# Attention scores as three float16 products instead of one float32 product, in a fused three-layer kernel

## The chip, the cores and the metric

One core of a Trainium2 chip runs the whole program. The metric is the device time of one execution in microseconds (us). The engines are TensorE (PE, with its weight loads listed as PEld), VectorE (DVE), ScalarE (ACT), GpSimd (POOL) and SyncE (SP), which issues the DMAs.

## What is computed

Three layers in a row, on 8 x 576 tokens of 512 features. First an attention in chunks of 64 tokens, 8 heads of 64; then a feed-forward layer; then a gated layer that mixes tokens. The first one, on which the change acts:

```python
scores = scale * np.matmul(q_c, k_c.transpose(0, 1, 2, 4, 3))
scores = scores - np.max(scores, axis=-1, keepdims=True)
attn = np.exp(scores)
attn = attn / (np.sum(attn, axis=-1, keepdims=True) + 1e-09)
out = np.matmul(attn, v_c)
```

The second layer normalizes a row of the result, multiplies by `w_ch1` (512 x 2048), applies a ReLU, multiplies by `w_ch2` (2048 x 512) and adds the row. The third does `w_in`, a GELU, a gate with `w_sg`, and `w_out`.

## The kernel before

Tokens are in 36 tiles of 128 rows, here called units, t = 0 to 35; two units make a block of the feed-forward layer (18 blocks). The program has two parts. The first does attention and feed-forward, block after block; its order comes from `Plan`: every operation is entered with an engine, a duration, what it reads and writes, a priority and a latency for its readers, and `Plan.run` lists them greedily, each engine at its earliest moment and by priority. What it lists is then the fixed order of each engine's queue; at run time each instruction waits on semaphores. The second part (the gated layer) has a plan of its own.

Operations with `two=1` hold off operations of the other engine of the pair DVE and POOL that carry `two` as well: the planner never lets a marked one of POOL overlap a marked one of DVE.

From unit 10 on (`JOIN`) attention runs inside the feed-forward blocks of two blocks earlier. Big matmuls are written as three float16 products of halves: high by high, high by low, low by high, where ACT rounds to the high half and DVE (or POOL) subtracts to get the low half. So it is with the second product of attention from unit 10 on (`pv_`, L341 to L356: 48 matmuls of 64x64). The scores, however, are float32: `scores` (L279) loads Q and K of a unit into `qkl` (one buffer, 128 x 1024 float32, L283), and `qk` (L286) issues 16 matmuls of 64x64, four at a time in the four quarters of TensorE. For units 10 to 34 `attention` enters `pv_` of unit t and `qk` of unit t+1 as one operation (L429), called a burst below; the scores of unit 10 stand alone (L317), and the second product of unit 35 does (L425).

Around a burst in the attention of a unit: the row maximum (L389) and the subtraction (L390) on DVE straight from PSUM, the exponential on ACT (L393), its high half (L400, ACT) and low half (L401, DVE), a DMA that transposes both halves (`ptt`, L404), the halves of V (`vq`, L408 ACT, L409 DVE), row sums (L413, L377, L378), then the next burst. After it, L430 scales the result into `x`, and `norm` (L439) normalizes it (L462, L463, POOL L457 and L460, L466), halves it into `hl` (L469 ACT, L471 POOL) and transposes it by DMA to `xT` (L267).

The feed-forward work in between, one of 8 steps of a block: 24 matmuls into a bank (`ff1p`, L750), a ReLU out of it on ACT (L765), sums on DVE (L772 to L774), the high half on ACT (L777), the low half on DVE (L778), and two steps later 21 matmuls (`ff2p`, L802) whose third one is the first to read the low half. At a block's end DVE (L825) and POOL (L835) add up the results. Between these the planner spreads the conversion of the third layer's weights (L491, L924, L987 on DVE), at the lowest priority.

Of the kernel before, what the change touches and what calls it, by code (L numbers as in the profile page):

```python
# [9 lines left out]
F16 = mybir.dt.float16  # L10
F32 = mybir.dt.float32
# [3 lines left out]
AF = mybir.ActivationFunctionType  # L15
ALU = mybir.AluOpType
# [8 lines left out]
    a=[2264, -1991, -1698, -26, -1734, 4025, 2562, -374],  # L25
# [4 lines left out]
    lo=[1, 0, 0, 0, 0, 1, 1, 1],  # L30
# [8 lines left out]
    xn=[0, 1, 0, 0, 1, 1, 1, 1],  # L39
    g=[150, 12000, 200, 400, 150],  # L40
    f=[-277, -1680, 2543],
# [9 lines left out]
JOIN = 10  # L51
# [96 lines left out]
def fused_kernel(ctx: ExitStack, tc, qkv, w1, w2, g1, w_in, w_out, wsgt, wsgs, g2, b_sg, out):  # L148
    nc = tc.nc
    PSUM = bass.MemoryType.PSUM  # L150
    P = 128
# [64 lines left out]
    op = plan.op  # L216
# [54 lines left out]
    def palloc(tag, bufs, shape, dt, pool=None):  # L271
        return plan.buf(tag, bufs, lambda: (pool or pools["att"][1]).tile(shape, dt, tag=tag, name=tag, bufs=bufs))
# [3 lines left out]
    started = {}  # L276
    BYDMA = 10

    def scores(t, o):  # L279

        a = palloc("qk", 2, [P, 2, 512], F32) if t < JOIN else palloc("qkl", 1, [P, 2, 512], F32)
        src = qkv[t].rearrange("p (a f) -> p a f", a=3)
        o("SP", 1700, lambda: nc.sync.dma_start(out=a.t, in_=src[:, 0:2]), wr=[a], lat=2200 if t < JOIN else 4000)  # L283
        s2 = pair[t % 2 if t < 6 else 1]

        def qk():  # L286
            for hp in range(4):
                for r in (slice(0, 64), slice(64, 128)):
                    for c in range(2):
                        k = hp * 128 + c * 64  # L290
                        nc.tensor.matmul(  # L291
                            s2[64 * c:64 * c + 64, r.start // 64, hp * 64:hp * 64 + 64],
                            lhsT=a.t[r, 0, k:k + 64],
                            rhs=a.t[r, 1, k:k + 64],
                            start=True,
                            stop=True,
                        )

        started[t] = a, qk

    def attention(t):
        n = t % 2 if t < 6 else 1
        s2, ks = pair[n], f"pair{n}"
        kp = ks if t < JOIN else "pairv"
        pr = TUNE['a'][t] if t < 8 else 10 * t
        lat = TUNE['g'][2] if t < 8 else 300 if t < JOIN else 600 if t < JOIN + 2 else 1000 if t < BYDMA else 400
        far = dict(lat=1500 if t < JOIN + 2 else 3000 if t < BYDMA else 1000) if t >= JOIN else {}
        z = 1

        def o(eng, ns, fn, **k):  # L310
            ns = FAST.get((eng, ns), ns)
            op(eng, ns, fn, prio=k.pop("prio", pr), lat=k.pop("lat", lat), **k)

        if t not in started:
            scores(t, o)
            a, qk = started[t]
            o("PE", 1260 * z, qk, rd=[a], wr=[ks])  # L317
        v = palloc("v", 2, [P, 512], F32) if t < JOIN else palloc("vl", 1, [P, 512], F32)
        o("SP", 730, lambda: nc.sync.dma_start(out=v.t, in_=qkv[t].rearrange("p (a f) -> p a f", a=3)[:, 2]), wr=[v], lat=2200)
        mx = palloc("mx", 2, [P, 2, 4, 1], F32)  # L320
        pm = palloc("pm", 2, [P, 4, 2, 64], F32) if t < JOIN else palloc("pml", 1, [P, 4, 2, 64], F32)
        sm = palloc("sm", 2, [P, 4, 2, 1], F32)
        rd = palloc("rd", 2, [P, 4, 2, 1], F32)
        pt = palloc("pt", 1, [P, 4, 128], F32) if t < BYDMA else None
# [7 lines left out]
        ptt, vq = [None], [None]  # L332
        pp = lambda: [pt, v] if t < BYDMA else [ptt[0], vq[0]]
# [7 lines left out]
        def pv_():  # L341
            if t >= BYDMA:
                for hp in range(4):
                    for n, (y, z) in enumerate(((0, 0), (0, 1), (1, 0))):
                        for r in (slice(0, 64), slice(64, 128)):
                            for c in range(2):
                                k = c * 256 + hp * 64
                                q = hp * 128 + c * 64
                                nc.tensor.matmul(  # L349
                                    s2[64 * c:64 * c + 64, r.start // 64, 256 + hp * 64:256 + hp * 64 + 64],  # L350
                                    lhsT=ptt[0].t[r, y, q:q + 64],
                                    rhs=vq[0].t[r, z, k:k + 64],
                                    start=(n == 0),
                                    stop=(n == 2),
                                )
                return  # L356
            for hp in range(4):
                for r in (slice(0, 64), slice(64, 128)):
                    for c in range(2):
                        k = c * 256 + hp * 64  # L360
                        nc.tensor.matmul(
                            s2[64 * c:64 * c + 64, r.start // 64, 256 + hp * 64:256 + hp * 64 + 64],
                            lhsT=pt.t[r, hp, 64 * c:64 * c + 64],
                            rhs=v.t[r, k:k + 64],
                            start=True,
                            stop=True,
                        )
# [12 lines left out]
        def sums():  # L380
# [10 lines left out]
            out=pm.t.rearrange("p h a k -> p a h k"), in0=sv, in1=mx.t.to_broadcast([P, 2, 4, 64]), op=ALU.subtract  # L391
# [4 lines left out]
        else:  # L396
            ph = palloc("ph", 1, [P, 2, 512], F16)
# [4 lines left out]
                out=ph.t[:, 1], in0=flat(), in1=ph.t[:, 0], op=ALU.subtract  # L402
            ), rd=[pm], wr=[ph], two=1)
            o("SP", 1100, lambda: nc.sync.dma_start_transpose(  # L404
                out=ptt[0].t.rearrange("p x (h q) -> p (x h) q", h=4), in_=ph.t.rearrange("p x f -> p (x f)")
# [4 lines left out]
                out=vq[0].t[:, 1], in0=v.t, in1=vq[0].t[:, 0], op=ALU.subtract  # L410
# [4 lines left out]
        if t < BYDMA:  # L415
            o("ACT", 480, lambda: nc.scalar.activation(
                out=pt.t.rearrange("p (a h) q -> p a h q", a=2),
                in_=s2[:, :, 0:256].rearrange("p a (h q) -> p a h q", h=2),
                func=AF.Copy,
# [4 lines left out]
        if t < JOIN or t + 1 == NT:  # L424
            o("PE", 1260 * z, pv_, rd=pp(), wr=[kp])  # L425
        else:
            scores(t + 1, o)
            a_, qk_ = started[t + 1]
            o("PE", 1260, lambda: (pv_(), qk_()), rd=pp() + [a_], wr=[kp, ks])  # L429
        o("DVE", 600, lambda: nc.vector.tensor_tensor(  # L430
            out=x.t.rearrange("p (h a d) -> p a h d", h=4, a=2),
            in0=pv,
            in1=rd.t.rearrange("p h a o -> p a h o").to_broadcast([P, 2, 4, 64]),
# [5 lines left out]
    def norm(t, x, o):  # L439

        bs = palloc("bs", 2, [P, 6], F32)
        mv = palloc("mv", 2, [P, 2], F32)
        rs = palloc("rs", 2, [P, 1], F32)
        xn = palloc("xn", 1, [P, 512], F32)
        hl = palloc("hl", 2, [P, 2, 512], F16)
        b = t // 2
        c0 = (t % 2 if b < B0 else 1 - t % 2) * 128
        if t % 2 == 0:
            if b == 2:
                xT_t[b] = plan.buf("xT2", 1, lambda: stage.tile([P, 2, 4, 256], F16, name="xT2"))  # L450
            else:
                xT_t[b] = palloc("xT", 2, [P, 2, 4, 256], F16, px)
        xT = xT_t[b]
        x_t[t] = x

        def rs_():
            nc.gpsimd.tensor_scalar(  # L457
                out=rs.t, in0=mv.t[:, 1:2], scalar1=1.0, scalar2=1e-6, op0=ALU.mult, op1=ALU.add
            )
            nc.gpsimd.tensor_tensor(out=rs.t, in0=rs.t, in1=cpow, op=ALU.pow)  # L460

        o("DVE", 600, lambda: nc.vector.bn_stats(out=bs.t, in_=x.t), rd=[x], wr=[bs])  # L462
        o("DVE", 70, lambda: nc.vector.bn_aggr(out=mv.t, in_=bs.t), rd=[bs], wr=[mv])  # L463
        o("POOL", 730, rs_, rd=[mv, "cpow"], wr=[rs], two=2)
        xe = ("POOL", 830, nc.gpsimd) if t < 8 and TUNE['xn'][t] else ("DVE", 460, nc.vector)
        o(xe[0], xe[1], lambda: xe[2].tensor_scalar(  # L466
            out=xn.t, in0=x.t, scalar1=mv.t[:, 0:1], scalar2=rs.t, op0=ALU.subtract, op1=ALU.mult
        ), rd=[x, mv, rs], wr=[xn], two=1 + (xe[0] == "POOL"))
        o("ACT", 520, lambda: nc.scalar.activation(out=hl.t[:, 0], in_=xn.t, func=AF.Copy), rd=[xn], wr=[hl])  # L469
        lo = ("DVE", 600, nc.vector) if t < 8 and TUNE['lo'][t] else ("POOL", 1110, nc.gpsimd)  # L470
        o(lo[0], lo[1], lambda: lo[2].tensor_tensor(  # L471
            out=hl.t[:, 1], in0=xn.t, in1=hl.t[:, 0], op=ALU.subtract
        ), rd=[xn], wr=[hl], two=1)
        o("SP", 1100, lambda: transpose(xT.t, slice(c0, c0 + 128), hl.t), rd=[hl], wr=[xT], lat=2200)
# [379 lines left out]

    bW = {"top": Buf("topB", None)}

    ATT = [f"{n}{k}" for n in ("qk", "v", "mx", "pm", "sm", "rd", "bs", "mv", "rs", "hl") for k in range(2)] + ["pt", "xn", "qkl", "vl", "u0", "u1", "pml", "ph", "ptt", "vq"]
    w2s = {}

    def open_sums():  # L860
# [822 lines left out]
```

## Time and profile before

| | us |
|---|---|
| median of 3 runs | 1175.69 (1175.21 to 1175.86) |
| the profiled execution's own time | 1174.16 |
| its span, first to last instruction | 1172.4 |
| PE busy in the span | 1160.4 (99%) |
| DVE, ACT, POOL busy | 921.5, 587.8, 200.6 |

The profiled execution took 1.53 us (0.13%) less than the median of the runs. A busy share is an average over stages; a wait counts only where the engine that waits is the one that sets the end. In the rows, a duration of a matmul overlaps the next one's, so what a batch of matmuls costs is read from the start of the batch to the start of what follows it.

### The profile page before, as it was taken

The page shows a single profiled execution, that of the slowest core. Times are in us where ns is not written, and L with a number is a line of the kernel's source. Part 1 is how long each engine was busy: PE and PEld are TensorE (multiplying, and loading weights), DVE is VectorE, ACT ScalarE, POOL GpSimd, SP SyncE. Part 2 cuts the span into 40 slices and gives each one's busy share as a digit, 9 for nine tenths or more (in the row PEclk, how much of TensorE's full clock was granted, in tenths as well). Part 3 has the DMA queues.
Part 4 walks back from the last instruction along what each step waited for, and adds up shares of the span by engine and source line. Part 5 has one row for each costly group of instructions (what it writes and reads, how often), then busy time and mean ns, then how long its engine had stood idle before and what let it go on. Part 6 is the DMA issues. An engine that isn't in the chain of part 4 may idle for free.

```text
span 1172.4 us, 28060 instructions
## 1 busy us (share of the span) xinstructions
PE 1160.4 (99%) x11858; PEld 880.5 (75%) x11858; DVE 921.5 (79%) x1752; ACT 587.8 (50%) x858; POOL 200.6 (17%) x279
## 2 busy tenths in 40 slices
PE   7999999999999999999999999999999999999998
PEld 5787448888888888888888888888565566556454
DVE  6997887989998998768877865677889579577455
ACT  5777635656565644434444443345646445434330
POOL 2211010212312222311311222012102001102100
PEclk8999999999999999999999999999999999999999
DMA  8973018454333444233233211436275463362203
GB/s 299 284 233 113 18 28 256 147 127 67 79 89 77 104 115 101 55 77 92 56 91 74 61 41 37 98 78 176 42 139 164 107 145 110 94 121 72 91 1 117
DMA packets 169278, 125.42 MB, mean 107 GB/s; under 512 B 132928, under 2 KB 142016, under 8 KB 169152
## 3 DMA queue, kind: packets, MB, share of 16 engines
q1 hardware_dynamic: 169152, 123.63, 40.5%
q8 instruction: 93, 1.52, 0.5%
q14 instruction: 33, 0.27, 0.1%
HBM read 72.74 MB, written 18.88 MB: 78 GB/s over the span
## 4 chain that ended last, share of the span: by engine, by line
PE 93%; DVE 3%; DMA 2%; ACT 1%; issue 1%; POOL 0%; SPq 0%; ACTq 0%; DVEq 0%; POOLq 0%
PE bank L750 25%; PE acc L802 22%; PE pb L1478 5%; PE bank L638 5%; PE acc L1562 4%; PE pair L659 4%; PE pb L1562 4%; PE acc L1478 3%; PE pb L1382 3%; PE pb L1424 3%; PE acc L1424 3%; PE acc L1382 3%; PE bank L659 2%; PE pair L291 2%; PE pair L349 1%; DMA xT<-hl 1%
## 5 line engine op out<-in xcount | busy, mean ns | idle before, releaser
L750 PE MATMUL bank<-xT,w1h 128*128 128x256 f16 x1920 | 320.9, 273 | 0.0
L802 PEld LDWEIGHTS <-arena 128*128 128x128 f16 x2520 | 244.1, 98 | 31.0 <-DVE arena L778 1.2
L750 PE MATMUL bank<-xT,w1l 128*128 128x256 f16 x960 | 261.8, 273 | 0.0
L802 PE MATMUL acc<-w,arena 128*128 128x256 f16 x1440 | 218.3, 273 | 0.6 <-DVE arena L778 0.6
L750 PEld LDWEIGHTS <-w1h 128*128 128x128 f16 x1920 | 187.7, 98 | 22.1
L777 ACT ACTIVATE arena<-arena 128x896 f16<-128x896 f32 x120 | 113.9, 949 | 144.1 <-PE acc L802 67.6
L802 PE MATMUL acc<-w2s,arena 128*128 128x256 f16 x1080 | 177.2, 273 | 0.0
L778 DVE TENSOR_TENSOR arena<-arena 128x896 f16<-128x896 f32 x120 | 132.1, 1101 | 36.7 <-ACT arena L777 36.4
L765 ACT ACTIVATE arena<-bank 128x512 f32<-128x512 f32 x120 | 71.3, 594 | 127.0 <-PE bank L750 124.0
L750 PEld LDWEIGHTS <-w1l 128*128 128x128 f16 x960 | 93.9, 98 | 10.9
L835 POOL TENSOR_TENSOR x<-x,u 128x256 f32<-128x256 f32 (+1 forms) x65 | 63.2, 998 | 174.9 <-ACT arena L777 107.7
L772 DVE TENSOR_TENSOR arena<-arena 128x256 f32<-128x256 f32 x120 | 57.2, 477 | 34.3 <-ACT arena L765 33.2
L1562 PEld LDWEIGHTS <-w2s 128*128 128x128 f16 x444 | 43.4, 98 | 47.3
L1382 PEld LDWEIGHTS <-x2T 128*128 128x128 f16 x672 | 65.5, 98 | 9.8
L638 PE MATMUL bank<-xT,w1h 128*128 128x256 f16 x384 | 64.4, 273 | 1.1 <-DMA xT<-hl 0.8
L457 POOL TENSOR_SCALAR rs<-mv 128x1 f32<-128x1 f32 x36 | 11.0, 306 | 312.9 <-DVE mv L463 283.5
L1424 PEld LDWEIGHTS <-late 128*128 128x128 f16 x336 | 32.7, 98 | 39.2
L773 DVE TENSOR_TENSOR arena<-arena 128x256 f32<-128x256 f32 x120 | 56.0, 467 | 4.1
L471 POOL TENSOR_TENSOR hl<-xn,hl 128x512 f16<-128x512 f32 x32 | 45.1, 1410 | 80.1 <-ACT hl L469 80.1
L1478 PEld LDWEIGHTS <-vh 128*128 128x128 f16 x288 | 28.6, 99 | 33.3
L1562 PE MATMUL acc<-wout,w2s 128*128 128x512 f16 (+1 forms) x252 | 53.3, 369 | 0.0
L638 PE MATMUL bank<-xT,w1l 128*128 128x256 f16 x192 | 52.3, 273 | 0.0
(283 smaller groups left out, 2098.1 us busy)
## 6 DMA issues: line engine op xcount, KB each, us to landing
straw<-in_w SPq DMA_DIRECT2D x16, 1023.8 KB, 5.5
qkl<-in_qkv SPq DMA_DIRECT2D x26, 512.0 KB, 4.1
x2d<-x SPq DMA_DIRECT2D x36, 256.0 KB, 2.0
xs<-x2d SPq DMA_DIRECT2D x27, 256.0 KB, 3.6
vl<-in_qkv SPq DMA_DIRECT2D x26, 256.0 KB, 3.0
w2s<-x2d SPq DMA_DIRECT2D x21, 256.0 KB, 2.8
out<-w2s SPq DMA_DIRECT2D x21, 256.0 KB, 3.0
qk<-in_qkv SPq DMA_DIRECT2D x10, 512.0 KB, 6.0
```

Source lines behind the costliest of these rows:

```text
L638: nc.tensor.matmul(acc, lhsT=w[j][:, k, fc], rhs=xT.t[:, x, k], start=(n == 0), stop=(n == 11))
L659: nc.tensor.matmul(acc[i], lhsT=h[x].t[:, c], rhs=w2t[j][:, f % 2, y], start=(f == 0 and n == 0), stop=(f == NF - 1 and n == 2),)
L750: nc.tensor.matmul(acc[:, y * 256:y * 256 + 256], lhsT=w[j][:, k, fc], rhs=xT.t[:, x, k], start=(n == 0), stop=(n == 11),)
L765: op("ACT", 500, lambda: nc.scalar.activation(out=o.t[:, 0:4].rearrange("p n t -> p (n t)"), in_=acc, func=AF.Relu, scale=0.5), rd=[kb] + ...
L777: op("ACT", 860, lambda: nc.scalar.activation(out=h.t[:, 0], in_=o.t[:, 1:8], func=AF.Copy), rd=[o] + ar, wr=[h], prio=-100)
L778: op("DVE", 1010, lambda: nc.vector.tensor_tensor(out=h.t[:, 1], in0=o.t[:, 1:8], in1=h.t[:, 0], op=ALU.subtract), rd=[o, h], wr=[h.key + ...
L802: nc.tensor.matmul(acc, lhsT=h.t[:, x, n], rhs=r(y), start=(first and j == 0 and m == 0), stop=(j == 7 and m == 2), skip_group_check=True,)
L835: op("POOL", ns, lambda: nc.gpsimd.tensor_tensor(out=d(), in0=d(), in1=v(), op=ALU.add), rd=u + ["q6", "q5", "q7"], wr=[x], prio=-50, two=1)
L1382: nc.tensor.matmul(ap[:, q * 256:q * 256 + 256], lhsT=xT[:, x, a, k, c], rhs=right(b, 1, k, w), start=(first and n == 0), stop=(k == 1 and ...
L1424: nc.tensor.matmul(ap, lhsT=right(b, 0, k, w)[:, m * 128:m * 128 + 128], rhs=xT[:, x, a, k], start=(first and n == 0), stop=(k == 1 and w ...
L1478: nc.tensor.matmul(ap, lhsT=v[:, fc], rhs=w[:, 0:512], start=(n == 0), stop=end)
L1562: nc.tensor.matmul(ap[:, 0:m], lhsT=x[:, k, c], rhs=w[:, k, fc], start=(n == 0), stop=(n == 11))
```

## The change

From unit 10 on, Q and K are split into float16 halves, `qh` by ACT and `ql` by POOL's subtraction, and the scores become three products of halves, 48 matmuls of 64x64 instead of 16 float32 ones. The buffer `hl` of these units becomes a single one, `hll`. The planner's latency of the load goes from 4000 to 5000.

```diff
     def scores(t, o):
 
-        a = palloc("qk", 2, [P, 2, 512], F32) if t < JOIN else palloc("qkl", 1, [P, 2, 512], F32)
+        far = t >= JOIN
+        a = palloc("qkl", 1, [P, 2, 512], F32) if far else palloc("qk", 2, [P, 2, 512], F32)
         src = qkv[t].rearrange("p (a f) -> p a f", a=3)
-        o("SP", 1700, lambda: nc.sync.dma_start(out=a.t, in_=src[:, 0:2]), wr=[a], lat=2200 if t < JOIN else 4000)
+        o("SP", 1700, lambda: nc.sync.dma_start(out=a.t, in_=src[:, 0:2]), wr=[a], lat=5000 if far else 2200)
         s2 = pair[t % 2 if t < 6 else 1]
+        parts = [(a, a)]
+        if far:
+            hi, lo = (palloc(n, 1, [P, 2, 512], F16) for n in ("qh", "ql"))
+            o("ACT", 1050, lambda: nc.scalar.activation(out=hi.t, in_=a.t, func=AF.Copy), rd=[a], wr=[hi], lat=600)
+            o("POOL", 2130, lambda: nc.gpsimd.tensor_tensor(
+                out=lo.t, in0=a.t, in1=hi.t, op=ALU.subtract
+            ), rd=[a, hi], wr=[lo], lat=1000, two=1)
+            parts = [(hi, hi), (hi, lo), (lo, hi)]
 
         def qk():
             for hp in range(4):
+                for n, (y, z) in enumerate(parts):
...
+                                lhsT=y.t[r, 0, k:k + 64],
+                                rhs=z.t[r, 1, k:k + 64],
+                                start=(n == 0),
+                                stop=(n + 1 == len(parts)),
...
-        hl = palloc("hl", 2, [P, 2, 512], F16)
+        hl = palloc("hl", 2, [P, 2, 512], F16) if t < JOIN else palloc("hll", 1, [P, 2, 512], F16)
```

What the planner makes of it moves instructions on all engines from unit 10 on; up to there, and in the second part, the queues are the same. In the rows below L299 and above keep their meaning with a shift: L349 of before is L359 in the changed kernel, L291 is L301, L802 is L812, L835 is L845, L471 is L481, L404 is L414.

On PE, around a burst in the middle of the attention (`pair_67` is the PSUM tile of scores and results, `acc_2375` one of `ff2p`'s), before:

```order
L349 LDWEIGHTS ptt
L349 MATMUL pair_67<-vq,ptt 64x64
L291 MATMUL pair_67<-qkl 64x64 [waits DMAHW7_49]
L291 MATMUL pair_67<-qkl 64x64 x15
L802 LDWEIGHTS arena [waits Activation_49]
L802 MATMUL acc_2375<-w_6_172,arena 128x256
```

and in the changed kernel:

```order
L359 LDWEIGHTS ptt
L359 MATMUL pair_67<-vq,ptt 64x64
L301 LDWEIGHTS qh
L301 MATMUL pair_67<-qh 64x64
...
L301 MATMUL pair_67<-ql,qh 64x64 [waits Pool_49]
...
L301 LDWEIGHTS ql
L301 MATMUL pair_67<-qh,ql 64x64
...
L812 LDWEIGHTS arena [waits Activation_49]
L812 MATMUL acc_2375<-w_6_172,arena 128x256
```

The 16 float32 matmuls have become 48 float16 ones with their weight loads, in the same place; the wait for the load of Q and K has become a wait for POOL.

On POOL, in the second half of the attention (`rs`, `hl` and `hll` belong to `norm`, `x` and `u` to the sums at a block's end), before:

```order
L460 TENSOR_TENSOR rs<-rs,cpow 128x1 [waits Pool_49]
L471 TENSOR_TENSOR hl<-xn,hl 128x512 [waits DMAHW0_49,Activation_49]
L835 TENSOR_TENSOR x<-x,u 128x512 [waits DMAHW2_49,DVE_49,Activation_49]
L835 TENSOR_TENSOR x<-x,u 128x256 [waits DMAHW3_49,DVE_49]
```

and in the changed kernel:

```order
L470 TENSOR_TENSOR rs<-rs,cpow 128x1 [waits Pool_49]
L481 TENSOR_TENSOR hll<-xn,hll 128x512 [waits DMAHW7_49,DVE_49,Activation_49]
L290 TENSOR_TENSOR ql<-qkl,qh 128x1024 [waits DMAHW5_49,Activation_49]
L845 TENSOR_TENSOR x<-x,u 128x256 [waits DVE_49]
L845 TENSOR_TENSOR x<-x,u 128x512 [waits DVE_49,Activation_49]
```

The subtraction for `ql` stands behind `norm`'s and ahead of the sums at the block's end; there is one for each of the 26 units.

On SP, in the same stretch, the load of Q and K and the transpose of the exponentials, before:

```order
L283 DMA qkl<-in_qkv 128x1024 [waits DMAHW6_49,DMAHW4_49,PE_49]
L319 DMA vl<-in_qkv 128x512 [waits DMAHW1_49,DMAHW5_49,DVE_49,Activation_49]
L404 DMA_TRANSPOSE ptt<-ph 128x8x128 [waits DMAHW0_49,DVE_49]
```

and in the changed kernel:

```order
L284 DMA qkl<-in_qkv 128x1024 [waits DMAHW5_49,DMAHW1_49,Pool_49]
L414 DMA_TRANSPOSE ptt<-ph 128x8x128 [waits DMAHW4_49,DVE_49,PE_49]
L267 DMA_TRANSPOSE xT<-hll 128x8x128 [waits DMAHW7_49,PE_49]
```

The load waited for PE's burst and now waits for POOL's subtraction, with the transpose behind it in the queue.

## Rows read from the trace of the kernel before

**Rows 1.** Page: busy time by engine, and PE's busy tenths and granted clock in 40 slices.

```profile
PE 1160.4 (99%) x11858; PEld 880.5 (75%) x11858; DVE 921.5 (79%) x1752; ACT 587.8 (50%) x858; POOL 200.6 (17%) x279
...
PE   7999999999999999999999999999999999999998
...
PEclk8999999999999999999999999999999999999999
```

**Rows 2.** Waits of PE, 180 us to the end: us in total, times, longest us.

```profile
PE acc L802 <- DVE arena L778: 0.6, 2, 0.5
```

**Rows 3.** Timeline of PE at 300 us, a burst: start us, us, engine, line.

```profile
300.41 0.58 PE L349 MATMUL pair<-vq,ptt 64*64 64x64 f16 x48
300.81 0.70 PE L291 MATMUL pair<-qkl 64*64 64x64 f32 x32
301.44 0.50 PE L802 MATMUL acc<-w,arena 128*128 128x256 f16 x3
```

**Rows 4.** Timeline of PE at 693 us, the last unit's second product, alone.

```profile
693.23 0.58 PE L349 MATMUL pair<-vq,ptt 64*64 64x64 f16 x48
693.74 0.50 PE L802 MATMUL acc<-w,arena 128*128 128x256 f16 x3
```

**Rows 5.** L291's and L349's instructions: ns min/median/max, first and last start us.

```profile
L291 PE MATMUL pair<-qkl x832: 217/219/267, 186.3 to 668.1; 64*64 64x64 f32 x167
L349 PE MATMUL pair<-vq,ptt x1248: 192/193/214, 200.4 to 693.6; 64*64 64x64 f16 x179
```

**Rows 6.** Groups of ACT and POOL instructions: busy us, mean ns, idle before.

```profile
L984 ACT ACTIVATE late<-tmp 128x1024 f16<-128x1024 f32 x8 | 8.4, 1055 | 0.2
L835 POOL TENSOR_TENSOR x<-x,u 128x512 f32<-128x512 f32 x13 | 16.5, 1267 | 173.9 <-ACT arena L777 107.7 <-DVE x L825 63.2 <-issue 3.0
```

**Rows 7.** POOL instructions of L471 and L835: ns min/median/max.

```profile
L471 POOL TENSOR_TENSOR hl<-xn,hl x32: 1153/1334/2276, 25.0 to 703.5; 128x512 f16<-128x512 f32 x32
L835 POOL TENSOR_TENSOR x<-x,u x65: 719/732/1543, 226.2 to 728.8; 128x256 f32<-128x256 f32 x52, 128x512 f32<-128x512 f32 x13
```

**Rows 8.** Busy us by stage: PE, PEld, DVE, ACT, POOL, clock, DMA share, GB/s.

```profile
180.00:303.00 123.00, 122.36 (x1563) 108.13 (x1562) 109.51 (x211) 77.25 (x113) 23.62 (x25) 1.00 0.56 143
303.00:429.00 126.00, 126.00 (x1644) 111.90 (x1642) 115.45 (x224) 73.68 (x104) 33.12 (x36) 1.00 0.38 93
429.00:720.00 291.00, 290.98 (x3546) 258.77 (x3545) 222.21 (x424) 124.81 (x180) 64.49 (x77) 1.00 0.29 71
```

**Rows 9.** The same stages, L291 alone: PE and PEld busy us.

```profile
180.00:303.00 123.00, 4.87 (x224) 4.08 (x224) 1.00 0.56 143
303.00:429.00 126.00, 4.87 (x224) 4.11 (x224) 1.00 0.38 93
```

**Rows 10.** Timelines of DVE and POOL at 208 us.

```profile
208.21 0.42 DVE L772 TENSOR_TENSOR arena<-arena 128x256 f32<-128x256 f32 x1
208.66 1.26 DVE L773 TENSOR_TENSOR arena<-arena 128x256 f32<-128x256 f32 x1
...
208.28 1.37 POOL L471 TENSOR_TENSOR hl<-xn,hl 128x512 f16<-128x512 f32 x1 [1.77 <-ACT hl L469]
```

**Rows 11.** Timelines of DVE, POOL and PE at 277 to 280 us.

```profile
277.64 3.05 DVE L778 TENSOR_TENSOR arena<-arena 128x896 f16<-128x896 f32 x2
...
277.51 1.22 POOL L471 TENSOR_TENSOR hl<-xn,hl 128x512 f16<-128x512 f32 x1 [2.79 <-ACT hl L469]
...
279.74 0.28 PE L802 MATMUL acc<-w,arena 128*128 128x256 f16 x1 [0.45 <-DVE arena L778]
```

**Rows 12.** Timelines of DVE and PE, a low half and its reader, 545 to 552 us.

```profile
545.66 1.09 DVE L778 TENSOR_TENSOR arena<-arena 128x896 f16<-128x896 f32 x1
...
552.07 0.49 PE L802 MATMUL acc<-w,arena 128*128 128x256 f16 x3
```

**Rows 13.** Timelines of SP and PE, a transpose and its burst; DMA issues: median us to landing.

```profile
537.51 1.45 SPq L404 DMA_TRANSPOSE ptt<-ph  x1
...
542.51 0.58 PE L349 MATMUL pair<-vq,ptt 64*64 64x64 f16 x48
...
ptt<-ph SPq DMA_TRANSPOSE x26, 3.3
```

**Rows 14.** DVE groups of 180 to 720 us: busy us, mean ns.

```profile
L389 DVE TENSOR_REDUCE mx<-pair 128x8 f32<-128x512 f32 x26 | 17.6, 678 | 3.5 <-PE pair L291 3.5
L390 DVE TENSOR_TENSOR pml<-pair,mx 128x512 f32<-128x512 f32 x26 | 17.5, 671 | 0.3
```

More of the change, by code (lines that the diff above doesn't have):

```diff
@@ L279, in scores @@
     def scores(t, o):
-        a = palloc("qk", 2, [P, 2, 512], F32) if t < JOIN else palloc("qkl", 1, [P, 2, 512], F32)
+        far = t >= JOIN
+        a = palloc("qkl", 1, [P, 2, 512], F32) if far else palloc("qk", 2, [P, 2, 512], F32)
         src = qkv[t].rearrange("p (a f) -> p a f", a=3)
-        o("SP", 1700, lambda: nc.sync.dma_start(out=a.t, in_=src[:, 0:2]), wr=[a], lat=2200 if t < JOIN else 4000)
+        o("SP", 1700, lambda: nc.sync.dma_start(out=a.t, in_=src[:, 0:2]), wr=[a], lat=5000 if far else 2200)
         s2 = pair[t % 2 if t < 6 else 1]
+        parts = [(a, a)]
[6 more added lines that the diff above has]
+            parts = [(hi, hi), (hi, lo), (lo, hi)]
         def qk():
             for hp in range(4):
[L288 to L299, printed above, removed]
+                for n, (y, z) in enumerate(parts):
+                    for r in (slice(0, 64), slice(64, 128)):
+                        for c in range(2):
+                            k = hp * 128 + c * 64
+                            nc.tensor.matmul(
+                                s2[64 * c:64 * c + 64, r.start // 64, hp * 64:hp * 64 + 64],
+                                lhsT=y.t[r, 0, k:k + 64],
+                                rhs=z.t[r, 1, k:k + 64],
+                                start=(n == 0),
+                                stop=(n + 1 == len(parts)),
+                            )
+        started[t] = [hi, lo] if far else [a], qk
     def attention(t):
@@ L316, in attention @@
             a, qk = started[t]
-            o("PE", 1260 * z, qk, rd=[a], wr=[ks])
+            o("PE", 1260 * z, qk, rd=a, wr=[ks])
         v = palloc("v", 2, [P, 512], F32) if t < JOIN else palloc("vl", 1, [P, 512], F32)
@@ L428, in attention @@
             a_, qk_ = started[t + 1]
-            o("PE", 1260, lambda: (pv_(), qk_()), rd=pp() + [a_], wr=[kp, ks])
+            o("PE", 1260, lambda: (pv_(), qk_()), rd=pp() + a_, wr=[kp, ks])
         o("DVE", 600, lambda: nc.vector.tensor_tensor(
@@ L855, in fused_kernel @@
     bW = {"top": Buf("topB", None)}
-    ATT = [f"{n}{k}" for n in ("qk", "v", "mx", "pm", "sm", "rd", "bs", "mv", "rs", "hl") for k in range(2)] + ["pt", "xn", "qkl", "vl", "u0", "u1", "pml", "ph", "ptt", "vq"]
+    ATT = [f"{n}{k}" for n in ("qk", "v", "mx", "pm", "sm", "rd", "bs", "mv", "rs", "hl") for k in range(2)] + ["pt", "xn", "qkl", "qh", "ql", "hll", "vl", "u0", "u1", "pml", "ph", "ptt", "vq"]
     w2s = {}
```

## The prediction

> **What bounds the kernel now.** I read the busy times first: PE is busy 1160.4 us of a span of 1172.4, at the full granted clock from the second slice on [rows 1]. A busy PE alone proves nothing, so the waits of PE come next: from 180 us to the end it waits for anything at all 0.6 us, twice, both times for the low half that DVE makes [rows 2]. So from 180 us on the time is the sum of what PE issues; a us taken out of PE's queue comes off the end, unless a new wait of PE takes it back. Whatever the change adds to ACT, POOL or SP costs nothing until it makes PE wait, and the two waits show the way by which that would come.
>
> The sum is made against the profiled execution, 1174.16 us, 1.53 below the median of the runs; I carry the difference over to the median, 1175.69. A measurement of this kernel can tell about 0.2% from no change, which is 2.35 us.
>
> **The change, part by part.**
>
> *Scores on PE.* In a burst, 48 float16 matmuls of the second product start at 300.41, the scores at 300.81, the next feed-forward matmul at 301.44 [rows 3]. So the scores cost 0.63 us from their start to what follows. What 48 float16 matmuls of the same shape cost is shown by the last unit, whose second product stands alone: 693.23 to 693.74, 0.51 us up to what follows [rows 4]. In the burst the same 48 take 0.40 up to the scores, so leaving the 64x64 shape for the 128x128 one costs 0.11 of the 0.51. The tempting sum is 0.63 - 0.40 = 0.23 us a unit, but it forgets that the exit, now paid behind the float32 scores, will be paid behind the new ones. I take 0.63 - 0.51 = 0.12 us. The bounds: rounded starts move it by 0.02 down; upward, the first matmuls of a float16 batch take up to 214 ns against a median of 193 [rows 5], some 0.02 us of entry that a second batch behind the first needn't pay again. So 0.10 to 0.14. The trace has 832 records of the float32 matmuls in batches of 32 [rows 3, 5], 26 units: 26 x 0.12 = 3.1 us, bounds 2.6 and 3.6.
>
> A rule of the Trainium skill speaks against this term. Its page TensorEngine Tiling (Array Packing), section Performance Considerations, says that each matmul carries about 60 cycles of overhead, so that small ones don't pay. By an estimate from that page, four quarters at a time and 64 + 60 cycles at 2.4 GHz, the 12 steps of 48 matmuls would take 0.62 us and the change would gain nothing; the row of the same shape says 0.40 before the exit, and the measurement decides.
>
> *ACT.* 26 roundings of 128x1024 to float16. The weights' conversion has that shape: 1.055 us [rows 6], so 27.4 us in all. ACT is busy 77.25 of 123 us in the fullest stage [rows 8]. In the queue the rounding stands just behind the one for `vq`, right after a burst; behind it waits the high half L777, which comes up to 1.06 us later, and with it L778. In the second half of the attention a low half is ready at 546.75, and its first reader is the third matmul of a batch that starts at 552.07: over 5 us to spare [rows 12]. Cost: nothing. If that cover were gone, 26 x 1.06 us would be the most.
>
> *POOL.* 26 subtractions of 128x1024. The nearest is L471 with half as many columns and the same types, 1.15 us at its fastest; 256 columns more cost L835 1.267 - 0.73 = 0.54 us [rows 6, 7]. So 1.15 + 2 x 0.54 = 2.2 us each, 58 us in all, on an engine that is busy 33 of 126 us in its fullest stage [rows 8]. POOL itself has room. But DVE has little: where POOL's L471 runs from 208.28, DVE's L773, a sum of two SBUF operands that else takes 0.42 us, takes 1.26 and ends with POOL's [rows 10]. A subtraction can thus take up to 2.2 us from DVE, or nothing, where DVE meanwhile does work that reads PSUM or one operand: the maximum and the subtraction of the scores, 0.68 and 0.67 us [rows 14], which come due just then.
>
> How much of it reaches PE? DVE is idle 13.5 us of 180 to 303 and 10.5 us of 303 to 429, but 68.8 us of 429 to 720 [rows 8]. L291's 224 records per stage are 7 batches, so 14 of the 26 subtractions fall before 429 [rows 9], at most 14 x 2.2 = 31 us against 24 us of idle time. The planner knows of the exclusion (`two=1`) and pushes the third layer's conversions, which nobody needs before the second part, into the emptier half. So I take 0.3 us of new waits of PE, half of the 0.6 it has now; the bounds are nothing, and the 31 - 24 = 7 us that would be left if every subtraction blocked DVE for its whole length and no conversion moved.
>
> *Load, buffers, queue.* The loads are as many and as large. `qh` and `ql` of the next unit are made right after a burst, one operation of ACT and one of POOL, some 3.3 us, while the score batches of the 26 units, 186.3 to 668.1, lie 19.3 us apart on average [rows 5]; the load now waits for POOL instead of PE, so it starts about 4 us later and still has a whole unit to land. A single `hll` waits for one transpose per unit. The scores of unit 10 come some 1.5 steps later, in front of a block that doesn't need them yet. These cost nothing as long as no transpose is late.
>
> Sum: -3.1 + 0.3 = -2.8 us, 1171.4 for the profiled execution, 1172.9 for the median.
>
> **Rivals.**
>
> *A: scattered waits of PE.* The 0.45 us wait at 279.74 is just this: POOL's L471 ran from 277.51 to 278.73, the two L778 of that moment took 3.05 us together, and PE stood [rows 11]. The change adds 26 POOL instructions twice as long, 14 of them in the stages where DVE has about a tenth of its time free [rows 8, 9]. With one in three of these costing PE what that one did, or two of them costing their 1 us, it takes 2 to 3 us back: 1175.0, no change. For it: the transposes of the exponentials have a margin too, 542.51 - 537.51 - 3.3 = 1.7 us [rows 13], and DVE's L401 is a two-operand subtraction, so a full block of 2.2 us goes past it. Against it: the planner, which left 0.6 us over 26 units as it was.
>
> *B: DVE becomes the bound in the first half.* If most subtractions block DVE for their whole length and conversions in its queue stand ahead of the low halves, 7 us of waits come up between 200 and 430 us, and the time is 1175.7 - 3.1 + 7 = 1179.6, slower. It decides as soon as the waits of PE reach 5.5 us. The same holds if POOL, kept off by DVE's back-to-back sums, ends late and SP stands at the load of Q and K with the transpose behind it.
>
> The Trainium skill, page SBUF — State Buffer, section Who interferes with whom, states it as a rule: a DVE instruction with two SBUF inputs and a GpSimd one that reads SBUF exclude each other for a whole instruction. By that rule alone B's 7 us follow; the trace agrees at 208 us.
>
> *C: the scores are no cheaper behind the second product.* If PE can't be fed 96 matmuls and weight loads in a row as fast as 48, the 0.12 shrinks: at a quarter more time per new batch nothing is left, and the time is 1175.7. The trace of before has no such run of short instructions to show it; the 48 of a burst cost less than the 16 behind them [rows 3].
>
> **How the numbers follow.** My forecast (gain 2.6 to 3.6, waits under 0.7 us): 0.52, with a range of its own of 1172.0 to 1173.6. A: 0.26, between 1173.6 and 1177. C: 0.07. B: 0.15, 1178 and above. Faster by over 0.2% means under 1173.3: the forecast nearly whole and a little of A and C, 0.52. Within 0.2%: the rest of A and C, 0.32. Slower: B and the far end of A, 0.16. The range of 8 in 10 runs from 1172.0 to 1177.5: it leaves out most of B and a little below.
>
> **What would show it.** In the changed profile: the scores as batches of 48 float16 records from whose start to the next feed-forward matmul 0.51 us pass; a whole burst of 0.91 instead of 1.03; `ql` at 2.2 us and `qh` at 1.06; DVE busier by blocked time, first in L773, L778 and L377; the waits of PE still under 1 us, all for L778 or `ptt`. The prediction is wrong if these waits sum to 3 us or more (A or B), which the waits of PE by stage would place before 430 us, or if a burst takes 1.0 us or more (C).

## The result, and the profile after

The changed kernel takes 1185.18 us (median of 6 runs, 1183.73 to 1188.45), the kernel before on the same chip 1175.45 (1173.76 to 1175.87). The ratio is 1.0091, 95% interval 1.0074 to 1.0108: slower by 0.9%, where 0.24% faster was forecast. The profiled execution took 1183.73 us, its span is 1181.9, 9.5 us more than before.

The page of the changed kernel, the row of busy times that answers to [rows 1], its share of instruction fetches, and the group of the new subtraction:

```profile
PE 1159.1 (98%) x12274; PEld 878.0 (74%) x12274; DVE 931.3 (79%) x1752; ACT 608.6 (51%) x884; POOL 257.9 (22%) x305
...
q8 instruction: 96, 1.57, 0.6%
...
L290 POOL TENSOR_TENSOR ql<-qkl,qh 128x1024 f16<-128x1024 f32 x26 | 57.8, 2222 | 72.8 <-ACT qh L289 60.1
```

PE's busy time fell by 1.3 us and the time rose by 9.5, so PE must be idle more. POOL's subtraction costs what the prediction said, 2.2 us. The timeline of PE at 337 us, a burst of the changed kernel, against [rows 3]:

```profile
337.21 0.58 PE L359 MATMUL pair<-vq,ptt 64*64 64x64 f16 x48
337.61 0.21 PE L301 MATMUL pair<-qh 64*64 64x64 f16 x4
...
338.15 0.50 PE L812 MATMUL acc<-w,arena 128*128 128x256 f16 x3
```

The second product still takes 0.40 us up to the scores, the scores 0.54 up to what follows them. On the mean of 25 units they take 0.533 us, where the float32 ones took 0.628, so a unit gains 0.095 us, and all 26 together 2.5. That part came nearly as forecast. The waits of PE from 180 us on, against the single row of [rows 2], and then the same stages as in [rows 8] (us, then PE, PEld, DVE, ACT, POOL, clock, DMA share, GB/s):

```profile
PE acc L812 <- issue: 2.9, 1, 2.9
PE acc L812 <- DVE arena L788: 2.7, 2, 2.5
PE bank L760 <- issue: 1.6, 1, 1.6
PE pair L359 <- DMA ptt<-ph: 0.8, 1, 0.8
PE acc L812 <- ACT arena L787: 0.5, 1, 0.5
```

```profile
180.00:303.00 123.00, 119.34 (x1556) 105.45 (x1554) 105.98 (x198) 72.49 (x104) 40.91 (x32) 0.99 0.51 148
303.00:429.00 126.00, 121.65 (x1703) 106.76 (x1701) 107.94 (x210) 73.62 (x106) 46.02 (x42) 0.99 0.38 80
429.00:720.00 291.00, 291.00 (x3835) 258.92 (x3833) 240.37 (x444) 147.61 (x210) 90.35 (x89) 1.00 0.32 73
```

PE waits 8.5 us instead of 0.6, nearly all before 429 us. DVE is *less* busy there than before (105.98 and 107.94 us against 109.51 and 115.45), so it doesn't bound the kernel there; from 429 to 720, where POOL does 12 of its 26 subtractions, PE doesn't wait at all. The largest wait has "issue" behind it: nothing that the profile shows was awaited. Here it is, in the timelines of PE and of SP:

```profile
259.51 0.57 PE L359 MATMUL pair<-vq,ptt 64*64 64x64 f16 x48 [0.78 <-DMA ptt<-ph]
...
260.44 0.50 PE L812 MATMUL acc<-w,arena 128*128 128x256 f16 x3
260.78 0.27 PE L812 MATMUL acc<-w2s,arena 128*128 128x256 f16 x1
263.94 0.59 PE L812 MATMUL acc<-w2s,arena 128*128 128x256 f16 x2 [2.89 <-issue]
```

```profile
253.11 1.25 SPq L414 DMA_TRANSPOSE ptt<-ph  x1
254.41 0.66 SPq L961 DMA_DIRECT2D redd<-redc  x1
255.32 1.23 SPq L267 DMA_TRANSPOSE xT<-hll  x1
```

PE stands in the middle of a batch of three. Just before, a transpose issued at 253.11 was awaited until 259.5, 6.4 us instead of its median of 3.3 [rows 13]. Between the two transposes stands a write that the prediction never looked at: `redd<-redc`, 128 values of the third layer's weight maxima, one from each partition, to a DRAM scratch, from where they are read back as a row.

The two other large waits are one event:

```profile
310.21 1.23 SPq L414 DMA_TRANSPOSE ptt<-ph  x1
...
312.12 0.45 SPq L961 DMA_DIRECT2D redd<-redc  x1
314.83 1.23 SPq L267 DMA_TRANSPOSE xT<-hll  x1
317.59 0.33 SPq L687 DMA_DIRECT2D x2d<-x  x1
```

```profile
326.19 0.69 DVE L440 TENSOR_TENSOR x<-pair,rd 128x512 f32<-128x512 f32 x1 [4.59 <-DMA x2d<-x]
...
327.53 1.07 DVE L788 TENSOR_TENSOR arena<-arena 128x896 f16<-128x896 f32 x1
```

Again a write of the same kind between two transposes. The stores of `x2d` behind it land at about 326 us, where 2.0 us is their median; L440, which overwrites what they read, waits 4.59 us for them; the low half L788 is queued behind L440, and PE waits 2.46 us for that (its 1.64 us of "issue" lie just before). After the waits PE's clock falls. The windows of the two stretches behind them:

```profile
263.90:266.60 2.70, 2.66 (x13) 1.93 (x14) 2.42 (x5) 1.33 (x2) 1.23 (x1) 0.50 0.00 0
...
328.60:331.60 3.00, 2.94 (x14) 2.04 (x15) 2.93 (x10) 1.55 (x2) 0.74 (x2) 0.50 0.00 0
```

The granted clock is 0.50 in both, the level of 1.2 GHz, after PE had stood for 2.89 and 2.46 us. 27 matmuls took 5.7 us there; at 0.11 us apiece (0.34 from 260.44 to 260.78 for three) they take 3.0, so 2.7 us were lost. The sum: 7.9 us of new waits and 2.7 of clock, less 2.5, is 8.1 of the 9.5. Another 0.6 us lies ahead of 180 us, where the queues of both kernels are the same: one and the same matmul starts there at 180.27 us before and at 180.83 after. 0.8 us I haven't assigned.

What does "issue" stand for? The trace also has records of the transfers that bring PE its instructions, in blocks of 16 KB: 96 of them, 1.57 MB for 12274 matmuls and as many loads, so about 64 bytes each and 256 to a block. From 180 to 740 us:

```
kernel     fetches  median   over 2 us (start: duration in us)
before     54       0.98     265.6: 3.40
changed    57       0.96     261.3: 3.22   304.9: 3.42   320.3: 2.54
```

One of the three slow ones begins within the stop of 261 us, one ends 0.2 us ahead of the stop of 323 us; the third (2 us behind the write issued at 302.83) lies on no stop, and in its time no transpose is in flight: the last one landed at 303.6, the next is issued at 310.2. The one of the kernel before begins 5.5 us behind a `redd` write issued at 260.07, and PE did not stop; no transpose is in flight there either.

### The profile page after: what moved, and what is told of

It is laid out like the page before. It is cut to its first block, busy times and chain, and to the rows that moved or that the text cites. A ratio compares the mean times of both kernels' runs of the same rounds, so it can differ in the third digit from the quotient of the medians.

```text
span 1181.9 us, 28960 instructions
## 1 busy us (share of the span) xinstructions
PE 1159.1 (98%) x12274; PEld 878.0 (74%) x12274; DVE 931.3 (79%) x1752; ACT 608.6 (51%) x884; POOL 257.9 (22%) x305
## 3 DMA queue, kind: packets, MB, share of 16 engines
q8 instruction: 96, 1.57, 0.6%
## 4 chain that ended last, share of the span: by engine, by line
PE 87%; DVE 6%; DMA 4%; ACT 1%; issue 1%; SPq 0%; POOL 0%; ACTq 0%; DVEq 0%; POOLq 0%
PE bank L760 24%; PE acc L812 21%; PE pb L1488 5%; PE acc L1572 4%; PE pair L669 4%; PE pb L1572 4%; PE acc L1488 3%; PE pb L1392 3%; PE bank L648 3%; PE acc L1434 3%; PE pb L1434 3%; PE acc L1392 3%; PE bank L669 2%; DMA straw<-in_w 1%; PE pair L301 1%
## 5 line engine op out<-in xcount | busy, mean ns | idle before, releaser
L812 PEld LDWEIGHTS <-arena 128*128 128x128 f16 x2520 | 245.6, 98 | 37.5 <-DVE arena L788 3.5
L760 PE MATMUL bank<-xT,w1l 128*128 128x256 f16 x960 | 261.8, 273 | 0.0
L812 PE MATMUL acc<-w,arena 128*128 128x256 f16 x1440 | 218.8, 274 | 3.2 <-DVE arena L788 2.7
L812 PE MATMUL acc<-w2s,arena 128*128 128x256 f16 x1080 | 178.5, 274 | 2.9 <-issue 2.9
L788 DVE TENSOR_TENSOR arena<-arena 128x896 f16<-128x896 f32 x120 | 133.8, 1116 | 32.0 <-ACT arena L787 31.5
L290 POOL TENSOR_TENSOR ql<-qkl,qh 128x1024 f16<-128x1024 f32 x26 | 57.8, 2222 | 72.8 <-ACT qh L289 60.1
L845 POOL TENSOR_TENSOR x<-x,u 128x256 f32<-128x256 f32 (+1 forms) x65 | 55.9, 892 | 73.8 <-DVE x L835 73.3
L481 POOL TENSOR_TENSOR hll<-xn,hll 128x512 f16<-128x512 f32 x26 | 36.1, 1388 | 136.7 <-ACT hll L479 136.7
L467 POOL TENSOR_SCALAR rs<-mv 128x1 f32<-128x1 f32 x36 | 17.2, 478 | 222.6 <-DVE mv L473 221.2
L1339 POOL TENSOR_SCALAR rs<-mv 128x2 f32<-128x2 f32 (+1 forms) x20 | 6.4, 320 | 260.4 <-DVE mv L1334 257.4
```

Of the source, the lines that this page charges most:

```text
L760: nc.tensor.matmul(acc[:, y * 256:y * 256 + 256], lhsT=w[j][:, k, fc], rhs=xT.t[:, x, k], start=(n == 0), stop=(n == 11),)
L788: op("DVE", 1010, lambda: nc.vector.tensor_tensor(out=h.t[:, 1], in0=o.t[:, 1:8], in1=h.t[:, 0], op=ALU.subtract), rd=[o, h], wr=[h.key + ...
L812: nc.tensor.matmul(acc, lhsT=h.t[:, x, n], rhs=r(y), start=(first and j == 0 and m == 0), stop=(j == 7 and m == 2), skip_group_check=True,)
```

## Experiments

Three theories stood against each other: **S**, the bursts of 192 instructions in 0.93 us let PE run out of instructions (a form of the prediction's C); **O**, the new order of the work does it, wherever that acts; **P**, POOL's subtraction shuts out DVE (the prediction's A and B). After four runs O was made definite as **R**, the column write beside the transposes, against **T**, the transposes or stores alone.

**1. The changed kernel again.** No edit.

> The changed kernel once more, for a second trace of it. In its first trace PE stopped three times between 258 and 329 us (2.89 us at 261, 1.64 at 323, 2.46 at 326), and after two of the stops its clock was halved for 2.5 to 3 us. Theory S (instruction supply: a burst now has 96 matmuls and 96 weight loads, 192 instructions in 0.93 us, and PE runs dry when the next fetch of instructions is late): stops of 1 to 3 us with no other engine behind them, right after bursts, but at other bursts than the first time, since the late fetches come by chance; 1182 to 1188. Theory O (the new order of the work in the first 200 us after the units change over): stops at the same places as before, behind DVE or a transfer; 1183 to 1187. Theory P (GpSimd's 26 subtractions shut DVE out): stops behind DVE just after a subtraction.

Measured 1186.66 us (4 runs), ratio 1.0095 (1.0077 to 1.0113). Its waits of PE from 180 us on:

```profile
PE bank L760 <- issue: 2.5, 1, 2.5
PE acc L812 <- DVE arena L788: 1.9, 2, 1.7
PE pair L359 <- DMA ptt<-ph: 1.7, 1, 1.7
PE acc L812 <- issue: 1.2, 1, 1.2
```

The same stops, and not by chance at other bursts: against S. Counting PE's records, the first "issue" stop came behind instruction 5851 of the records in the first trace, 5845 here, and 5851 in run 3; the second behind 7425, 7426 and 7422, while the times differ by up to 3 us. A stop bound to a place in the instruction stream, with a fetch of 2.5 to 3.2 us under way or just over, looks like an empty instruction buffer. The times of the fetches don't show it, though: here PE goes on at 263.85 us, 2.5 us before the fetch that began at 263.19 is over.

**2. High half only, in the changed order.**

```diff
-            parts = [(hi, hi), (hi, lo), (lo, hi)]
+            parts = [(hi, hi)]
-                out=lo.t, in0=a.t, in1=hi.t, op=ALU.subtract
+                out=lo.t[:, 0, 0:1], in0=a.t[:, 0, 0:1], in1=hi.t[:, 0, 0:1], op=ALU.subtract
```

> The changed kernel's order of work, word for word, with ACT's high half in full; GpSimd's subtraction is cut to one column and the scores are one product of the high halves (16 matmuls and 16 loads for 48 and 48), so the low halves' part of the scores is left out. PE's own time falls by about 26 x (0.533 - 0.18) = 9 us against the changed kernel. S: no stop after a burst any more, the lost 10 to 12 us come back too: 1163 to 1166. P: the same, 1163 to 1166. O: the stops stay, 1174 to 1177.

Measured 1178.51 us (10 runs, 1170.48 to 1182.59), ratio 1.0014 (0.9993 to 1.0034), against 1163 to 1166 by S and P; O's 1174 to 1177 is missed too, by 1.5 us. The scores took 0.24 us a unit where the expectation had 0.18, which moves all of these numbers up by 1.6. Its waits of PE from 180 us on, in the profiled execution, the fastest of the ten:

```profile
PE bank L760 <- issue: 5.6, 2, 4.6
```

A burst has 128 instructions here, fewer than before the change (160 in the trace, where the 16 float32 matmuls are 32 records with as many loads), and POOL has next to nothing to do; the stops stay, up to 4.6 us long, and that one begins 0.3 us after the slow fetch beside it has ended. The first comes behind instruction 5597, 254 earlier than 5851: about one block of 256, though in another batch of matmuls.

**3. Three products, no subtraction.** GpSimd's operation is cut as in run 2, and

```diff
-            parts = [(hi, hi), (hi, lo), (lo, hi)]
+            parts = [(hi, hi), (hi, hi), (hi, hi)]
```

> The changed kernel's order, with three products of the high half with itself (96 matmuls and 96 loads in a burst as in the changed kernel) and GpSimd's subtraction cut to one column: the low half is left out. S: as the changed kernel, 1182 to 1188. O: the same, 1182 to 1188. P: the stops are gone, 1172 to 1174.

Measured 1182.71 us (5 runs), ratio 1.0058 (1.0038 to 1.0078).

```profile
PE acc L812 <- issue: 3.2, 1, 3.2
PE bank L760 <- issue: 2.0, 1, 2.0
PE acc L812 <- DVE arena L788: 1.8, 1, 1.8
```

The stops need no subtraction: P falls. Some 4 us less than in run 1, with intervals that just touch, may be POOL's; its trace lacks the waits for `ptt` at 259 us (0.8 and 1.7 us in the two traces of the changed kernel). I didn't pursue it.

**4. The old order with 96 + 96 instructions a burst.** In the kernel before, the 16 float32 matmuls of a burst become 48, of which the first keeps `a.t`:

```diff
-                            lhsT=a.t[r, 0, k:k + 64],
-                            rhs=a.t[r, 1, k:k + 64],
+                                    lhsT=a.t[r, 0, k:k + 64] if f else pt_.t[r, y, k:k + 64],
+                                    rhs=a.t[r, 1, k:k + 64] if f else vq_.t[r, z, k:k + 64],
```

> The kernel before, its order word for word, no split at all; only the 16 float32 matmuls of the scores in a burst are 48 matmuls (47 float16 on the halves that the second product reads, one float32 to keep the wait for the load), so that a burst has the changed kernel's 96 matmuls and 96 loads. The scores are then not those of the reference. S: loses like the changed kernel, 1180 to 1188. O and P: gains 0.095 us for each of 26 units, 1172.5 to 1173.5.

Measured 1176.56 us (10 runs), ratio 1.0011 (0.9999 to 1.0022). Neither number: S's is missed by 3.4 us, but the gain of 2.5 us isn't there either. The trace shows why:

```profile
301.37 0.25 PE L294 MATMUL pair<-qkl 64*64 64x64 f32 x1
...
302.00 0.50 PE L817 MATMUL acc<-w,arena 128*128 128x256 f16 x3
```

With the one float32 matmul among them, the 48 take 0.63 us up to what follows, as long as the scores of the kernel before, so there was nothing to gain and the expectation's 0.095 us a unit was wrong. The profiled execution (1174.65 us) has no wait of PE at all from 180 us on, with two fetches over 2 us. So the number of instructions in a burst doesn't make the stops by itself.

That left the order. In the changed kernel's queue of SP all three `redd` writes stand within 2.3 us behind a transpose, two of them with another 0.9 and 2.7 us behind them. In the kernel before:

```profile
257.42 1.23 SPq L267 DMA_TRANSPOSE xT<-hl  x1
...
260.07 0.89 SPq L951 DMA_DIRECT2D redd<-redc  x1
```

and the row of its DMA issues:

```profile
redd<-redc SPq DMA_DIRECT2D x3, 0.5 KB, 9.4
```

They take 9.4 us to land (median). This one comes 2.6 us behind a transpose, the other two 16.4 and 12.1 us, and the next transposes are 6.9, 18.7 and 9.3 us away.

**5. A row for the column.**

```diff
-nc.sync.dma_start(out=redd[i], in_=redc[:, i:i + 1])
+nc.sync.dma_start(out=row, in_=ident[0:1, 0:P])
```

> The changed kernel's order on every engine. The three writes of a 128x1 column of weight maxima to a DRAM scratch (redd<-redc, 128 pieces of 4 bytes, 9 us from issue to landing) become writes of one row of 512 bytes from a constant tile, so the scale of the weights is a fixed one and not their maximum. Theory R (such a write, issued between DMA transposes in the new order, makes the DMA engines slow for some us; PE's next fetch of instructions, 0.96 us otherwise, takes 2.5 to 3.4 us, and PE stands at the end of its block): no slow fetch from 255 to 325 us, no stop, 1172 to 1174.5. Theory T (the transposes by themselves, or the stores of x2d, are what delays the fetch): stops as in the changed kernel, 1182 to 1188. Theory S (192 instructions in a burst): stops too, 1182 to 1188.

Measured 1174.21 us (10 runs, before 1176.80), ratio 0.9987 (0.9976 to 0.9999). No stop in the stretch and no fetch over 2 us. With every other instruction in its place, 1.0% of the time, some 12 us, is gone (1.0091 in the first comparison, 0.9987 here): R; T and S fall. The row comes from a constant, so this write no longer waits for the maxima; run 10 keeps them.

**6 and 7. The writes moved in SP's queue.** One number of the planner; 0 in run 6, and 12000 in its place in run 7:

```diff
-rd=[f"mxc{i}"], wr=[f"redc{i}"], prio=pr, lat=4000)
+rd=[f"mxc{i}"], wr=[f"redc{i}"], prio=pr, lat=0)
```

> The changed kernel with one number of the planner changed (the assumed delay of the weight maxima, 4000 to 0): the work of PE, DVE, ACT and GpSimd keeps its order, and on the DMA queue two of the three column writes go three to five places earlier, the first before a load of queries and a load of values and no longer between two transposes, the second and third next to each other, behind the two transposes near 300 us. R: the stop at 263 us goes, and the third write's slow stretch (317 to 329 us) too, while the place near 303 us gets worse; 1174 to 1180. T and S: as the changed kernel, 1182 to 1188.

> The same number set to 12000: again only the DMA queue's order differs. The first write goes behind the second transpose at 256 us, the second and third some places later (behind the transposes of 310 to 315 us, and behind the stores of x2d). R: the slow stretches move with the writes; the total lies between, 1175 to 1184. T and S: as the changed kernel, 1182 to 1188, with the stops where they were.

Measured 1184.29 us, ratio 1.0071 (1.0048 to 1.0093), and 1188.62, ratio 1.0100 (1.0077 to 1.0123): no better, so R's numbers for both were missed. But the stops changed their kind with the places. Run 6, SP at 251 us, then the transpose's landing time among the DMA issues of 250 to 275 us, then PE:

```profile
251.25 0.33 SPq L961 DMA_DIRECT2D redd<-redc  x1
...
255.16 1.23 SPq L414 DMA_TRANSPOSE ptt<-ph  x1
```

```profile
ptt<-ph SPq DMA_TRANSPOSE x1, 10.4
```

```profile
265.57 0.64 PE L359 MATMUL pair<-vq,ptt 64*64 64x64 f16 x32 [4.55 <-DMA ptt<-ph]
```

The transpose that starts 3.9 us behind the write lands after 10.4 us, and PE waits for that one openly; "issue" stops are gone. In run 7 the write was issued at 256.83, 1.3 us behind a transpose with none behind it for 25 us, and PE stood 3.0 us with "issue" again. Its longest wait is of the other kind, behind the two writes of 313 and 317 us and the stores of `x2d` between them, for which L440 waits 6.6 us:

```profile
PE acc L812 <- DVE arena L788: 5.4, 1, 5.4
```

So it isn't being *between* transposes that hurts, as I had put it, but being in flight together with what PE needs: here from 1.3 us behind a transpose to 3.9 us ahead of one.

**8, 9, 12. The suspected cost, 26 times over.** In the kernel before, behind each DMA transpose of the exponentials one more write, of a constant column (run 8) or of a constant row (run 9); in run 12 the column again, but behind the 26 loads of Q and K.

```diff
+                nc.sync.dma_start(out=redx[t], in_=cpow)
```

```diff
+                nc.sync.dma_start(out=redx[t].rearrange("p n -> n p"), in_=ident[0:1, 0:P])
```

> The kernel before, its order kept; behind each of the 26 DMA transposes of the probabilities one more write of a 128x1 column of a constant to a DRAM scratch of its own (128 pieces of 4 bytes, read by nobody). R: slow fetches (over 2 us) behind many of the 26, some of them with a stop of PE of 1 to 4 us and a halved clock behind it: 1185 to 1230. T and S: no more than the queue's 0.4 us each, 1175 to 1178.

> The control to the 26 column writes: the kernel before, its order kept, with 26 more writes at the same places, behind the DMA transposes of the probabilities, but each of one row of 512 bytes (one piece) of a constant. R (it is the 128 pieces of 4 bytes that disturb): 1175 to 1178, no slow fetch beyond those of the kernel before. If any further write behind a transpose costs that much: 1185 to 1230.

> The kernel before, its order kept, with the same 26 extra column writes (128 pieces of 4 bytes), but behind the 26 loads of queries and keys and no longer behind the transposes. In the kernel before's trace these loads are issued 4 to 7 us behind a transpose in most cases (1.6 us in one) and 4 to 10 us ahead of the next, where the earlier run had 18 of 26 within 1.5 us behind one. Theory O (what costs is a column write and a DMA transpose in flight together): most of the 52 us go, 1178 to 1200, and the waits that are left are for transposes issued 4 us behind a write. Theory A (each column write costs 2 us wherever it stands): 1215 to 1235.

| run | us (runs) | ratio, 95% interval | fetches over 2 us |
|---|---|---|---|
| 8, columns behind transposes | 1229.19 (4) | 1.0436 (1.0396 to 1.0476) | 17 of 50 |
| 9, rows behind transposes | 1175.54 (10) | 1.0000 (0.9990 to 1.0010) | 1 of 54 |
| 12, columns behind loads | 1195.49 (4) | 1.0178 (1.0158 to 1.0198) | 10 of 53 |

26 writes of 512 bytes cost 52 us as columns and nothing as rows; the one slow fetch of run 9 begins with one of the kernel's own three column writes. Behind the loads the columns cost 20. The waits of PE in run 8 from 180 to 760 us and in run 12 from 180 to 740:

```profile
PE pair L350 <- DMA ptt<-ph: 15.7, 6, 4.2
PE acc L807 <- DVE u L830: 4.4, 2, 3.9
PE acc L807 <- DVE arena L783: 4.4, 2, 3.2
PE acc L807 <- issue: 4.2, 4, 1.3
PE bank L755 <- issue: 4.1, 2, 2.4
```

```profile
PE pair L355 <- DMA ptt<-ph: 13.0, 6, 7.5
PE acc L808 <- DVE u L831: 2.1, 1, 2.1
```

Run 12 has slow fetches too, and not one "issue" stop. So a slow fetch alone doesn't stop PE, as the slow one of the kernel before already showed. Nor does every "issue" stop have a fetch beside it: of the seven of run 8, four (at 211.1, 261.4, 507.0 and 592.1 us, 1.0 to 2.4 us long) have none within 1 us, neither slow nor quick. What PE lacks in these stops is open.

Run 12 also tells how far a column write reaches (its expectation calls O what is R here, and O's range held; A, 2 us for each write wherever it stands, fell). Its 26 writes take 9.7 us to land (median, 8.5 to 13.8). A transpose issued 3.3 us behind one took 9.1 us, at 4.7 us 7.9, at 7.0 us 6.1, and at 14.5 us 3.0, the undisturbed time. The longest wait, 7.5 us, is for a transpose issued 10.8 us behind a write that took 13.8: what counts is that the write is still under way.

**10 and 11. The mending.** Behind each maximum DVE transposes the column in 32x32 blocks, and the write is 4 pieces of 128 bytes; run 10 on the changed kernel, run 11 on the kernel before.

```diff
+            nc.vector.transpose(out=redt, in_=redc[:, i:i + 1].to_broadcast([P, 32]))
-nc.sync.dma_start(out=redd[i], in_=redc[:, i:i + 1])
+nc.sync.dma_start(out=redd[i].rearrange("(b j) n -> b (j n)", b=4), in_=redt[0:P:32])
```

> The changed kernel with the real maxima, and without the column writes: behind each of the three maxima DVE transposes the column in blocks of 32x32 (one instruction more, into a tile of 32 columns), and the write to the DRAM scratch takes 4 partitions of 32 values, 4 pieces of 128 bytes. Nothing is left out and the planner's numbers are the changed kernel's. R: no slow fetch and no stop between 250 and 330 us; 1172 to 1174.5, 0.1 to 0.35 % under the kernel before. T and S: as the changed kernel, 1182 to 1188.

> The kernel before with the same mending of its three writes, to tell what the split of the scores is worth by itself. R: in the kernel before no transpose starts within 7 us behind a column write, so nothing is won; 1174 to 1177, no difference that can be measured. If the writes cost it something too: 1170 to 1174, and the split's gain is the difference to the run above, 2 to 3 us expected.

Run 10: 1173.95 us (12 runs), ratio 0.9983 (0.9972 to 0.9994), faster than both kernels, than the one before by 0.2%, with nothing left out. Run 11: 1174.95 (11 runs), 0.9991 (0.9982 to 1.0000). The trace of run 10, SP's queue at the place of the first stop, the landing of its transpose, and the waits of PE from 180 us on:

```profile
254.18 1.91 SPq L415 DMA_TRANSPOSE ptt<-ph  x1
256.14 0.64 SPq L966 DMA_DIRECT2D redd<-redt  x1
256.88 1.26 SPq L268 DMA_TRANSPOSE xT<-hll  x1
```

```profile
ptt<-ph SPq DMA_TRANSPOSE x1, 4.0
```

```profile
PE acc L813 <- ACT arena L788: 0.6, 1, 0.6
PE acc L813 <- DVE arena L789: 0.3, 1, 0.3
```

The write still stands between the same two transposes. In 4 pieces it disturbs neither them nor a fetch (none of 57 over 2 us), and PE's waits are 0.9 us. The split is then worth 1174.95 - 1173.95 = 1.0 us; the two intervals overlap, so anything from nothing to the 2.5 us of the trace fits. The traces tell it more closely. The matmul near 180 us, with the same work ahead of it in all of them, starts anywhere from 180.0 to 183.8 us; counted from its start to that of the last matmul, it is 988.6 us before, 988.3 in run 9 and 988.1 in run 11, but 986.4 in run 5 and 986.7 in run 10. That is a gain of 1.4 to 2.2 us.

The Trainium skill, page DMA: Bandwidth & Descriptors, section Rules for kernel authors, says: "A transpose next to ordinary DMAs needs nothing". It stands in a rule on serializing transposes from different queues, against wrong data. In time it doesn't hold here: 10.4 us for a transpose behind a column write, 52 us for 26 such writes. The same page's section Specifications has transfers under 512 bytes done as read-modify-write; 128 pieces of 4 bytes fit that, but 4 pieces of 128 bytes lie under it too and cost nothing here.

## Why the prediction was wrong

*What bounds the kernel now: right.* New waits of PE from 180 us on moved the end later, and without them, in runs 5 and 10, most of the gain came off the end.

*Scores on PE: right in kind, just under the lower bound in size.* 0.095 us a unit where 0.12 was taken and 0.10 was the lower bound; 2.5 us for 3.1. The exit behind the new scores was paid, with 0.533 us instead of 0.51 for batch and exit. Rival C is out: no burst was slower.

*ACT, POOL: right in price.* 1.04 us a rounding, 2.22 us a subtraction, and PE waits for nothing in the stage that holds 12 of the 26. Rivals A and B named DVE, shut out by POOL, as the way into a loss. Run 3 takes the subtraction away and keeps the stops; DVE is less busy in the first half than before the change, not more. The subtraction does take time from DVE (931.3 us busy, 911.4 in run 3), but PE's waits are much the same without it, 7.3 us in run 3 and 7.8 in run 1; the 4 us between these runs may be its price. A's other way, the transposes' margin of 1.7 us, was taken: the one of 253.11 came 3.1 us late, but not by POOL. The size of B (slower, by 4 us) was nearer to the result than the forecast, by luck, as the mechanism is another.

*The step that failed: "Load, buffers, queue", with "These cost nothing as long as no transpose is late."* Transposes became late, and I had priced the queue by the change's own transfers alone. The change gave the planner new durations, and with them another order of SP's queue, in which a write that the change doesn't touch fell beside the transposes. Its replacement is measured: some 12 us for three such writes (a ratio of 1.0091 with them, 0.9987 and 0.9983 without). It hits by three ways: a late transpose, a late store with DVE queued behind it, and stops of PE with nothing awaited, with a halved clock behind two of the stops. "So I take 0.3 us of new waits of PE" is the number that this broke: 7.9 us. Two things in the trace of the kernel before could have warned: the 9.4 us of a 512-byte write, and a fetch of 3.4 us behind it that happened to do no harm.

Shown by taking it away and by multiplying it: the column write as the cause. Argued from records alone, and not borne out by run 8: that the "issue" stops are PE without instructions. Open: what stops PE there, by what the writes slow the other transfers, and the 4 us between runs 1 and 3.

## What to carry to other kernels

When a change goes through a planner, compare the DMA queue too, with the transfers that it doesn't touch: a kernel can owe its time to an order that happens to keep two transfers apart. Look for writes of one small element per partition, which a landing time far above that of larger transfers betrays, and turn them into a few long pieces before judging anything else. A wait of the bound engine with nothing behind it calls for a look at every transfer in flight just then, instruction fetches among them.

## What the runs showed of the hardware

A write of 128 pieces of 4 bytes took 9.4 us to land (median of 3 in the kernel before), and up to 13.8 in run 12. DMA transposes in flight with one took 6.4 us (changed kernel) to 10.4 us (run 6), where 3.3 is the median; of the fetches of 16 KB of PE's instructions, 0.96 us at the median in the changed kernel, 27 of 103 took over 2 us in runs 8 and 12 together, the longest 6.3; two in the first two traces did so with no transpose in flight. With the same 512 bytes in four pieces the transpose took 4.0 us, and in one piece or four no fetch was slow. PE stood 0.6 to 4.6 us with no semaphore to wait for (runs 8 and 2), in three traces within 6 instructions of the same place. After waits of 2.89 and 2.46 us (the second one for DVE) its granted clock was 0.50 in the windows of 2.7 and 3.0 us behind them.
